# Expert places ordered by token counts, with rooms of 448, 416 or 384 tokens, in 26 blocks instead of 28

## The chip, the core and the metric

The kernel runs on one NeuronCore of a Trainium2 chip. TensorE multiplies matrices into PSUM, VectorE and ScalarE work elementwise, GpSimd works elementwise and also issues the indirect transfers (rows picked by a list of indices), SyncE issues most plain transfers. The engines run beside each other and wait for each other by semaphores. The metric is the device time of one execution in microseconds, the median of several. Lower is better.

## What is computed

A gated linear attention is followed by a mixture of experts, in which each token goes to the one expert with the largest logit:

```python
# attention, (B, H, S, D) = (4, 8, 768, 48); its output is x, 3072 tokens of 384 numbers
state = alpha[:, :, t, :, None] * state + np.einsum('bhd,bhe->bhde', k[:, :, t], v[:, :, t])
y[:, :, t] = np.einsum('bhd,bhde->bhe', q[:, :, t], state)

# experts, N, D, E, F = (3072, 384, 8, 1024)
logits = x @ w_gate
expert_idx = np.argmax(logits, axis=1)
...                                    # probs = softmax(logits)
gate_w = probs[np.arange(N), expert_idx]
for e in range(E):                     # over the tokens of expert e
    h = np.maximum(x_sorted[lo:hi] @ w1[e], 0.0)
    y_sorted[lo:hi] = h @ w2[e]
y = y_sorted[inv_perm]
return gate_w[:, None] * y
```

All of it is float32. How many tokens an expert gets is known only when the logits are there, on the chip.

## The kernel before

The attention goes through 24 blocks of 128 tokens. Each block's rows and logits go to a table `x_rows` in memory. Beside it the kernel finds each token's expert and its slot, a number that says where in the experts' rows the token stands. A pair of experts shares 7 blocks of 128 slots: the first expert fills them from the front, the second from the back, each with room for 448 tokens, so the middle block is half of one and half of the other. A slot is cut into its row (0 to 127) and its column (the block), each made into a one-hot, and a matmul of the two writes the token's number where its slot is:

```python
    EP = E // 2; NJ = 7; HB = C // 2; CAP = NJ * HB      # C = 128: CAP = 448
    NX = -(-(N - CAP) // C); PB = NX + NJ + NX; NC = EP * PB   # NC = 196 columns

    def one_hots(s, eng=nc.vector):
        rc = st[s]["rc"]
        eng.tensor_scalar(oh_r[:, s, :], iota_h[:, :C], scalar1=rc[:, 0, :], scalar2=None, op0=ALU.is_equal)
        eng.tensor_scalar(oh_c[:, s, :], iota_h[:], scalar1=rc[:, 1, :], scalar2=tokv[:, s : s + 1],
                          op0=ALU.is_equal, op1=ALU.mult)

    def tokens_of_slots(t0, t1):
        for t in range(t0, t1):
            nc.tensor.matmul(route[:, :NC], lhsT=oh_r[:, t, :], rhs=oh_c[:, t, :], ...)

    def indices():
        tv = route[:, :NC]
        nc.vector.tensor_scalar_add(g_mid[...], tv[... NX : NX + NJ], float(N // 2))
        ...                                     # g_idx (all columns) and o_idx (rows of the output)
```

Between the last attention block and the first expert stand these steps. `keep_busy(n)` is n matmuls on zeros, whose result nobody reads:

```python
        one_hots(hots.pop(0), nc.gpsimd)
        one_hots(hots.pop(0))
        tokens_of_slots(9, NT - 3)
        slots_of(*rank_products(groups_of[-1], ...))
        tokens_of_slots(NT - 3, NT - 1)
        keep_busy(3)
        one_hots(hots.pop(0))
        tokens_of_slots(NT - 1, NT)
        nc.tensor.matmul(route[:, NC : NC + E], lhsT=ones_sq[:], rhs=ohs[:, NT, :], ...)
        keep_busy(8)
        indices()
```

Then the experts. A gather brings 128 rows of a block, `turn` transposes them on TensorE and VectorE copies them into `xT`, layer 1 multiplies with `w1` over the whole room of the expert, and layer 2 multiplies block by block with `w2`. The result is scaled by the gate and scattered to the output:

```python
    def products1(w1, xT, hp, f, c0, c1):
        for a in range(DB):                                   # DB = 3
            nc.tensor.matmul(hp[:, c0:c1], lhsT=w1[:, a, f * C : (f + 1) * C], rhs=xT[:, a, c0:c1], ...)

    def layer1(w1, xT, cols, begun=(), c0=0, then=None):      # cols = CAP
        h = wk.tile([C, FB, CAP], F32, name="h_sb")
        for f in range(FB):                                   # FB = 8
            hp = ...                                          # one of 3 PSUM tiles
            products1(w1, xT, hp, f, ..., cols)
            ...                                               # relu, VectorE for even f, ScalarE for odd f

    def layer2(parts, gw, idx, apart):
        zp = mps.tile([C, Dm], F32, name="zp")
        m = C // len(parts)                                   # 128, or 64 in the shared block
        for f in range(FB):
            for i, (w2, h, c0) in enumerate(parts):
                nc.tensor.matmul(zp[i * m : (i + 1) * m, :], lhsT=h[:, f, c0 : c0 + m], rhs=w2[:, f, :], ...)
        ...                                                   # scale on ScalarE, scatter on GpSimd

    xg = gather(columns(0))
    for p in range(EP):
        a, b = 2 * p, 2 * p + 1
        ...                                                   # fetches of weights, gather of the next pair
        ha = layer1(w_t[a][0], xTa, CAP, begun, 2 * C)
        for j in range(NH + 1, NJ):                           # NH = 3
            turn(xg, j, (xTb, HB + (j - NH - 1) * C, 0, C))
        gw = gates(xg, NJ)
        for j in range(NH):
            layer2([(w_t[a][1], ha, j * C)], gw[:, j : j + 1], idx[j], True)
        hb = layer1(w_t[b][0], xTb, CAP)
        ...                                                   # turns of the next pair; for p == 0 extra_blocks()
        layer2([(w_t[a][1], ha, NH * C), (w_t[b][1], hb, 0)], gw[:, NH : NH + 1], idx[NH], True)
        for j in range(NH + 1, NJ):
            layer2([(w_t[b][1], hb, HB + (j - NH - 1) * C)], gw[:, j : j + 1], idx[j], True)
```

`extra_blocks` works out, on VectorE, how many tokens don't fit into their expert's room; a loop at the end runs once per block of such tokens.

Of the kernel before, what the change touches and what calls it, by code (L numbers as in the profile page):

```python
# [8 lines left out]
F32 = mybir.dt.float32  # L9
# [9 lines left out]
def kernel(  # L19
# [24 lines left out]

    nc = tc.nc
    B, H, S, D = q.shape
    C = 128
# [13 lines left out]
    EP = E // 2  # L61
    NJ = 7
    HB = C // 2
    CAP = NJ * HB

    NX = -(-(N - CAP) // C)
    PB = NX + NJ + NX
    NC = EP * PB

    W = Dm + E  # L70

    ends = list(range(0, NT - 7, 4)) + [NT - 5, NT - 3, NT - 1, NT]
    groups_of = [range(a, b) for a, b in zip(ends, ends[1:])]

# [43 lines left out]
    zero_w = consts.tile([1, W], F32)  # L118
    iotas = {}
    for name, shape, dt, pattern, base, mult in (  # L120

        ("first_w", [C, E], F32, [[-1, E]], E, 0),
        ("iota_h", [C, NC], F16, [[1, NC]], 0, 0),

        ("tokv", [C, NT], F32, [[N // 2 + 1, 2], [C, NT // 2]], -(N // 2), 1),
        ("sgn", [C, E], F32, [[0, EP], [2, 2]], -1, 0),
        ("slot0", [C, E], F32, [[PB * C, EP], [1, 2]], NX * C + CAP - 1, 0),

        ("base2", [C, E], F32, [[2 * PB, EP], [0, 2]], 2 * NX + NJ, 0),
        ("thr", [C, NX], F32, [[C, NX]], CAP, 0),  # L130
        ("kx", [1, NX], F32, [[1, NX]], 0, 0),
        ("xcol", [1, E], F32, [[PB, EP], [NJ + 1, 2]], NX - 1, 0),
    ):
        iotas[name] = (
            consts.tile(shape, I32, name=name + "_i"), consts.tile(shape, dt, name=name), pattern, base, mult,
        )
    first_w, iota_h, tokv, sgn, slot0, base2, thr, kx, xcol = (iotas[n][1] for n in iotas)

    def late_consts(i):
# [10 lines left out]
        if i in (2, 3, 4):  # L150
            for ti, tf, pattern, base, mult in list(iotas.values())[3 * (i - 2) : 3 * (i - 1)]:
                nc.gpsimd.iota(ti[:], pattern=pattern, base=base, channel_multiplier=mult)
                nc.gpsimd.tensor_copy(tf[:], ti[:])
            if i == 3:
                nc.gpsimd.tensor_scalar_mul(ohs[:, 0, :], base2[:], 0.5)
                first = ohs[0:1, 0, :].rearrange("p (a b) -> p a b", b=2)[:, :, 0]
                nc.gpsimd.tensor_scalar_add(first, first, -1.0)
            if i == 2:

                nc.sync.dma_start(x_d[N // 2 : N // 2 + 1, :], zero_w[:])  # L160

# [10 lines left out]

    g_mid = rte.tile([C, EP * NJ], I32)
    g_idx = rte.tile([C, NC], I32)
    o_idx = rte.tile([C, NC], I32)
    tot = rte.tile([C, E], F32)
# [38 lines left out]
    with tc.tile_pool(name="ld", bufs=6) as ld, \  # L215
# [35 lines left out]
        def cums(s):  # L251
            d = st[s]
            cum = ps.tile([C, Dm], F32, name="cum")
# [124 lines left out]
        def choose(g):  # L378
# [8 lines left out]

            if n == 1:
                nc.vector.scalar_tensor_tensor(
                    oh[:, t, :], in0=sc[:], scalar=top[:], in1=sgn[:, None, :], op0=ALU.is_equal, op1=ALU.mult,  # L390
                )
            else:
                nc.vector.tensor_tensor(sc[:], sc[:], top[:].unsqueeze(2).to_broadcast([C, n, E]), op=ALU.is_equal)
                nc.vector.tensor_tensor(oh[:, t, :], sc[:], sgn[:, None, :].to_broadcast([C, n, E]), op=ALU.mult)
# [10 lines left out]
        def slots_of(g, pos):  # L405
# [4 lines left out]
            slot_i = work.tile([C, n], I32, name="slot_i")  # L410
            with nc.allow_low_precision("a single number is not zero, and it is an integer"):
                nc.vector.tensor_reduce(slot_i[:], own[:], axis=AX, op=ALU.add, apply_absolute_value=True)
            rc_i = work.tile([C, 2, n], I32, name="rc_i")
            nc.vector.tensor_scalar(rc_i[:, 0, :], slot_i[:], scalar1=C - 1, scalar2=None, op0=ALU.bitwise_and)
            nc.vector.tensor_scalar(rc_i[:, 1, :], slot_i[:], scalar1=7, scalar2=None, op0=ALU.arith_shift_right)
            rc = work.tile([C, 2, n], F32, name="rc")
            nc.vector.tensor_copy(rc[:], rc_i[:])
            for i, s in enumerate(g):
                st[s]["rc"] = rc[:, :, i : i + 1]
                hots.append(s)  # L420

        def one_hots(s, eng=nc.vector):
            rc = st[s]["rc"]
            eng.tensor_scalar(oh_r[:, s, :], iota_h[:, :C], scalar1=rc[:, 0, :], scalar2=None, op0=ALU.is_equal)
# [12 lines left out]
        def indices():  # L437

            tv = route[:, :NC]
            nc.vector.tensor_scalar_add(  # L440
                g_mid[:].rearrange("p (a b) -> p a b", a=EP),
                tv.rearrange("p (a b) -> p a b", a=EP)[:, :, NX : NX + NJ], float(N // 2),
            )
            nc.vector.tensor_scalar_add(g_idx[:], tv, float(N // 2))
            up = [work.tile([C, NC], F32, name="up") for _ in range(2)]
            nc.vector.tensor_scalar(up[0][:], tv, scalar1=0.0, scalar2=-1.0, op0=ALU.is_gt, op1=ALU.mult)
            nc.vector.tensor_scalar(up[1][:], tv, scalar1=0.0, scalar2=float(N), op0=ALU.is_equal, op1=ALU.mult)
            nc.vector.tensor_tensor(up[0][:], up[0][:], up[1][:], op=ALU.add)
            nc.vector.scalar_tensor_tensor(
                o_idx[:], in0=tv, scalar=float(N // 2), in1=up[0][:], op0=ALU.add, op1=ALU.add,  # L450
            )
# [65 lines left out]
        route = ps.tile([C, Dm], F32, name="cum")  # L517
# [11 lines left out]
        tokens_of_slots(NT - 3, NT - 1)  # L529
        keep_busy(3)  # L530
        one_hots(hots.pop(0))
        tokens_of_slots(NT - 1, NT)
# [4 lines left out]
        indices()  # L537
        nc.vector.tensor_copy(tot[:], route[:, NC : NC + E])
# [6 lines left out]

    def extra_blocks():

        cnt = sm.tile([C, E], F32)
        nc.vector.tensor_tensor(cnt[:], tot[:], slot0[:], op=ALU.subtract)
        nc.vector.tensor_tensor(cnt[:], cnt[:], sgn[:], op=ALU.mult)  # L550
        og = sm.tile([C, E, NX], F32)
        nc.vector.tensor_tensor(
            og[:], cnt[:].unsqueeze(2).to_broadcast([C, E, NX]), thr[:, None, :].to_broadcast([C, E, NX]), op=ALU.is_gt,
        )
        ovt = sm.tile([C, E], F32)
        nc.vector.reduce_sum(ovt[:], og[:], axis=AX)
        ove = sm.tile([C, E], F32)
        nc.vector.tensor_tensor_scan(ove[:], ovt[:], zero_e[:], 0.0, op0=ALU.add, op1=ALU.add)
        ovs = sm.tile([1, E], F32)
        nc.vector.tensor_sub(ovs[:], ove[0:1, :], ovt[0:1, :])  # L560
# [11 lines left out]
        nth = sm.tile([1, NX, E], F32)  # L572
        nc.vector.tensor_tensor(nth[:], kx_b, per(ovs), op=ALU.subtract)
        live = sm.tile([1, NX, E], F32)
        nc.vector.tensor_scalar(live[:], nth[:], scalar1=0.0, scalar2=None, op0=ALU.is_ge)
        nc.vector.tensor_tensor(live[:], live[:], ended[:], op=ALU.subtract)
        nc.vector.tensor_tensor(nth[:], nth[:], per(sgn), op=ALU.mult)
        nc.vector.tensor_tensor(nth[:], nth[:], per(xcol), op=ALU.add)
        nc.vector.tensor_tensor(nth[:], nth[:], live[:], op=ALU.mult)
        nc.vector.reduce_sum(xf[:, NX : 2 * NX], nth[:], axis=AX)  # L580
# [3 lines left out]
    def gather(idx, n=0, later=False):  # L584

        xg = xg_pools[n % 2].tile([C, len(idx), W], F32, name="xg")
        if later:

            nc.vector.memset(xg[:, 0, :1], 0.0)
        for j, i in enumerate(idx):  # L590
            nc.gpsimd.indirect_dma_start(  # L591
# [36 lines left out]
    def layer1(w1, xT, cols, begun=(), c0=0, then=None):  # L628
        h = wk.tile([C, FB, CAP], F32, name="h_sb")
        for f in range(FB):  # L630
# [6 lines left out]
            if f == 0 and then:  # L637
                done = then()
        return (h, done) if then else h
# [129 lines left out]
```

## Time and profile before

| | |
|---|---|
| time, median of 3 | 473.68 us (472.63 to 473.82) |
| span of the profiled execution | 473.3 us |
| TensorE busy | 452.8 us (96%), 2919 matmul instructions |
| VectorE, ScalarE, GpSimd busy | 144.7, 106.0, 141.2 us |
| layer 2 (L647), busy | 146.8 us, 512 matmul instructions |
| layer 1 (L620), busy | 145.9 us, 402 matmul instructions |
| gathers (L591), scatters (L653) | 28 and 28 |
| moved by DMA | 59.79 MB |

In the profile's lines PE is TensorE's matmuls, PEld its loads of weights, DVE VectorE, ACT ScalarE, POOL GpSimd, SP SyncE; L620 is line 620 of the kernel. Shapes are partitions x elements, xcount is how many instructions a line stands for, and a bracket at the end of a timeline's line is how long the engine sat idle before it and what ended that. PEclk is the share of full clock that TensorE was granted. The lengths of matmuls overlap, as they are pipelined: the pace is read from start to start.

### The profile page before, as it was taken

To read this page: it belongs to the slowest core of one execution; us is meant where nothing else is said; L and a number is where in the kernel's file an instruction comes from. 1 tells how busy PE (TensorE), PEld (TensorE's weight loads), DVE (VectorE), ACT (ScalarE), POOL (GpSimd) and SP (SyncE) were. 2 spreads that over 40 slices of the span, in tenths; PEclk is the share of its full clock that TensorE was granted. 3 is DMA by queue.
4 is the path that set the end of the run, shared out by engine and by line. 5 is a ranking of instruction groups with operands and counts; after the bars stand their busy time and mean duration, and the time that the engine had idled before them with its cause. 6 is when DMAs were issued, how large, how long until landed. Compare 5 with 4: busy or idle time off the path is not lost.

```text
span 473.3 us, 7538 instructions
## 1 busy us (share of the span) xinstructions
PE 452.8 (96%) x2919; PEld 294.2 (62%) x2919; DVE 144.7 (31%) x412; ACT 106.0 (22%) x209; POOL 141.2 (30%) x228
## 2 busy tenths in 40 slices
PE   8999999999997899999999999999999999999992
PEld 5787887888886765554555555555555554555451
DVE  2646776767776312015013012001201101201000
ACT  3554554555531011010011010010110001111100
POOL 4567565556643500250160100133010010010020
PEclk9999999999999999999999999999999999999998
DMA  9999999999433404974473202634400230000000
GB/s 163 190 197 189 207 198 204 214 210 206 102 102 119 116 5 171 392 268 145 172 227 103 86 18 81 218 123 151 144 33 1 67 115 13 1 21 17 1 35 26
DMA packets 128687, 59.79 MB, mean 126 GB/s; under 512 B 110624, under 2 KB 123460, under 8 KB 128650
## 3 DMA queue, kind: packets, MB, share of 16 engines
q1 hardware_dynamic: 116258, 48.87, 41.1%
q0 software_dynamic: 3584, 10.34, 6.5%
q10 hardware_dynamic: 8808, 0.08, 1.1%
q8 instruction: 24, 0.39, 0.4%
q14 instruction: 13, 0.11, 0.1%
HBM read 49.70 MB, written 10.35 MB: 127 GB/s over the span
## 4 chain that ended last, share of the span: by engine, by line
issue 48%; PE 29%; POOL 10%; DMA 4%; DVE 3%; SPq 3%; ACTq 1%; ACT 1%; POOLq 0%
POOL out_dram L653 5%; PE hp L620 4%; POOL xg L591 4%; PE sA L298 4%; PE xr L365 3%; PE tp L285 3%; PE zp L647 3%; PE cum L254 3%; PE y L335 2%; PE y L328 2%; DMA x_rows<-xs 2%; DMA k_sb<-in_k_dram 2%; SPq L233 2%; PE kvp L335 2%; PE kvp L344 1%
## 5 line engine op out<-in xcount | busy, mean ns | idle before, releaser
L647 PE MATMUL zp<-w,h_sb 128*128 128x384 f32 (+1 forms) x512 | 146.8, 488 | 0.0
L620 PE MATMUL hp<-xT,w 128*128 128x448 f32 (+2 forms) x402 | 145.9, 523 | 0.6 <-DVE xT L616 0.6
L647 PEld LDWEIGHTS zp<-w,h_sb 128*128 128x128 f32 (+1 forms) x512 | 81.2, 177 | 62.3 <-issue 13.6
L620 PEld LDWEIGHTS hp<-xT,w 128*128 128x128 f32 x402 | 75.7, 190 | 68.3 <-issue 65.0
L653 POOL DMA_INDIRECT out_dram<-zo,o_idx x28 | 27.8, 992 | 246.9 <-ACT zo L652 246.9
L634 DVE TENSOR_SCALAR h_sb<-hp 128x448 f32<-128x448 f32 x32 | 20.0, 625 | 218.3 <-PE hp L620 206.7
L636 ACT ACTIVATE h_sb<-hp 128x448 f32<-128x448 f32 x32 | 17.4, 545 | 139.8 <-PE hp L620 131.9
L652 ACT ACTIVATE zo<-zp,gw 128x384 f32<-128x384 f32 x28 | 16.3, 582 | 133.5 <-PE zp L647 128.9
L591 POOL DMA_INDIRECT xg<-x_rows,g_mid x28 | 27.0, 966 | 12.9 <-issue 7.3
L298 PE MATMUL sB<-qT,kT 48*128 48x128 f32 x192 | 27.7, 285 | 0.0
L298 PE MATMUL sA<-qT,kT 48*128 48x128 f32 x192 | 27.7, 284 | 0.0
L285 PEld LDWEIGHTS tp<-ident,kqb 128*128 128x128 f32 x192 | 22.4, 140 | 7.2 <-issue 4.2
L277 POOL TENSOR_TENSOR kqb<-k_sb,icp 128x384 f32<-128x384 f32 x24 | 24.0, 1002 | 9.5 <-ACT icp L257 7.5
L365 PE MATMUL xr<-back,yT 128*128 128x104 f32 x192 | 25.1, 273 | 0.0
L285 PE MATMUL tp<-ident,kqb 128*128 128x128 f32 x192 | 24.9, 273 | 0.0
L254 PE MATMUL cum<-ln,cmask 128*128 128x384 f32 x48 | 22.0, 540 | 3.0 <-ACT ln L243 2.9
L298 PEld LDWEIGHTS sA<-qT,kT 48*128 48x128 f32 x192 | 23.1, 187 | 2.0 <-issue 0.5
L278 POOL TENSOR_TENSOR kqb<-q_sb,cp 128x384 f32<-128x384 f32 x24 | 24.1, 1003 | 0.0
L365 PEld LDWEIGHTS xr<-back,yT 128*128 128x128 f32 x192 | 23.3, 192 | 0.1
L298 PEld LDWEIGHTS sB<-qT,kT 48*128 48x128 f32 x192 | 23.1, 187 | 0.0
L305 POOL TENSOR_SCALAR_AFFINE_SELECT dB<-dB 128x512 f32<-128x512 f32 x24 | 15.3, 637 | 22.7 <-ACT dB L304 22.7
L616 DVE COPY xT<-xtp 128x384 f32<-128x384 f32 (+1 forms) x32 | 14.9, 504 | 21.8 <-PE xtp L614 21.8
(138 smaller groups left out, 456.1 us busy)
## 6 DMA issues: line engine op xcount, KB each, us to landing
w<-in_moe_w_dram SPq DMA_DIRECT2D x14, 1536.0 KB
x_rows<-xs SPq DMA_DIRECT2D x24, 196.0 KB
a_sb<-in_alpha_dram SPq DMA_DIRECT2D x24, 192.0 KB
k_sb<-in_k_dram SPq DMA_DIRECT2D x24, 192.0 KB
q_sb<-in_q_dram SPq DMA_DIRECT2D x24, 192.0 KB
vb<-in_v_dram SPq DMA_DIRECT2D x24, 192.0 KB
w<-in_moe_w_dram SPq DMA_DIRECT2D x12, 128.0 KB
w<-in_moe_w_dram SPq DMA_DIRECT2D x8, 192.0 KB
```

The source lines that it names most:

```text
L254: nc.tensor.matmul(cum[:], lhsT=cmask[:], rhs=d["ln"][:], start=True, stop=True)
L277: nc.gpsimd.tensor_tensor(kq[:, 0, :, :D], d["k"][:], heads(d["icp"]), op=ALU.mult)
L278: nc.gpsimd.tensor_tensor(kq[:, 1, :, :D], d["q"][:], heads(d["cp"]), op=ALU.mult)
L285: nc.tensor.transpose(tp[:, p, :], pair(kqb[s % 4][:, i], p), ident[:])
L298: nc.tensor.matmul(t[:, p, :], lhsT=d["kT"][r : r + D, p, :], rhs=d["qT"][r : r + D, p, :], start=True, stop=True,)
L335: nc.tensor.matmul(yp(p)[at(p, a) : at(p, a) + DP, :], lhsT=d["v"][:, 2 * p + a, :], rhs=d["d" + "AB"[a]][:, p, :], start=(c == 0 and p % ...
L365: nc.tensor.matmul(xr[:, p, :], lhsT=d["yT"][:, p, :], rhs=back[:, p, :], start=True, stop=True)
L591: nc.gpsimd.indirect_dma_start(out=xg[:, j, :], out_offset=None, in_=x_d[:, :], in_offset=bass.IndirectOffsetOnAxis(ap=i, axis=0),)
L620: nc.tensor.matmul(hp[:, c0:c1], lhsT=w1[:, a, f * C : (f + 1) * C], rhs=xT[:, a, c0:c1], start=(a == 0), stop=(a == DB - 1), skip_group_c ...
L634: nc.vector.tensor_relu(h[:, f, :cols], hp[:, :cols])
L647: nc.tensor.matmul(zp[i * m : (i + 1) * m, :], lhsT=h[:, f, c0 : c0 + m], rhs=w2[:, f, :], start=(f == 0), stop=(f == FB - 1), skip_group_ ...
L653: ins = nc.gpsimd.indirect_dma_start(out=out[:, :], out_offset=bass.IndirectOffsetOnAxis(ap=idx, axis=0), in_=zo[:], in_offset=None, bound ...
```

## The change

Instead of pairs with 448 slots for everyone, the eight experts get places in a row, with rooms of 448, 384, 448, 384, 416, 416, 416 and 416 slots: 3328 slots, which are 26 blocks of 128. Expert 0 has the first place; the other seven are put into the places by the order of their token counts, which the chip takes from the ranks after 19 of the 24 blocks (`turns`). The aim is fewer empty slots to compute. As the rooms are multiples of 32, a slot is cut into units of 32, and a block can belong to two experts in parts of 64 and 64 or of 32 and 96. Layer 2 then cuts a shared block into tiles of the smaller part. Which expert stands in a place is read from memory into a register, of SyncE for the fetches of weights and of VectorE for the indices. The diff, cut to what matters:

```diff
-    EP = E // 2
-    NJ = 7
-    HB = C // 2
-    CAP = NJ * HB
+    UN = 32
+    NQ = C // UN
+    NU = 16
+    NC = E * NU
+    caps = (448, 384, 448, 384, 416, 416, 416, 416)
+    nth_of = (5, 0, 6, 1, 2, 3, 4)
+    begins = [sum(caps[:i]) for i in range(E + 1)]
+    NBK = begins[-1] // C
...
+        def turns(first):
+            key = ...                    # count * 8 + tie, of experts 1 to 7, on one partition
+            ...                          # stand = how many have a larger key, by a 7 x 7 comparison
+            nc.vector.tensor_reduce(order_i[:], cmp[:], axis=AX, op=ALU.add)
...
         def one_hots(s, eng=nc.vector):
-            eng.tensor_scalar(oh_r[:, s, :], iota_h[:, :C], scalar1=rc[:, 0, :], scalar2=None, op0=ALU.is_equal)
+            eng.tensor_scalar(oh_r[:, s, :], iota_r[:], scalar1=rc[:, 0, :], scalar2=None, op0=ALU.is_equal)
...
-        def indices():
...
+        def slots(i):
+            b, n = begins[i] // UN, caps[i] // UN
+            tv = route[:, :NC].rearrange("p (e k q) -> p e k q", e=E, q=NQ)
+            e = nc.vector.value_load(order_i[0:1, i - 1 : i], min_val=1, max_val=E - 1) if i else 0
+            for q in range(NQ):
+                ...
+                to, src = g_idx[r, k : k + m], tv[r, bass.ds(e, 1), :m, u]
+                if i == 0 and q % 2:
+                    nc.scalar.activation(to, src, AF.Copy, bias=float(N // 2))
+                else:
+                    nc.vector.tensor_scalar_add(to, src, float(N // 2))
...
         tokens_of_slots(9, NT - 3)
         slots_of(...)
-        tokens_of_slots(NT - 3, NT - 1)
-        keep_busy(3)
+        keep_busy(4)
         one_hots(hots.pop(0))
-        tokens_of_slots(NT - 1, NT)
+        tokens_of_slots(NT - 3, NT)
         nc.tensor.matmul(route[:, NC : NC + E], ...)
         keep_busy(8)
-        indices()
+        slots(0)
...
     def layer2(parts, gw, idx, apart):
-        m = C // len(parts)
+        wd = C if len(parts) == 1 else min(m for *_, m in parts)
+        cuts = [(w2, h, c) for w2, h, c0, m in parts for c in range(c0, c0 + m, wd)]
         for f in range(FB):
-            for i, (w2, h, c0) in enumerate(parts):
-                nc.tensor.matmul(zp[i * m : (i + 1) * m, :], lhsT=h[:, f, c0 : c0 + m], ...)
+            for i, (w2, h, c) in enumerate(cuts):
+                nc.tensor.matmul(zp[i * wd : (i + 1) * wd, :], lhsT=h[:, f, c : c + wd], ...)
...
+    lots = [range(a, b) for a, b in ((0, 7), (7, 13), (13, 20), (20, NBK))]
+    def weights1(i, later=False):
+        nos[i] = nc.sync.value_load(order_i[0:1, i - 1 : i], min_val=1, max_val=E - 1)
+        w1n[i] = fetch1(nos[i], later)
+    ended = [range(begins[i] // C, begins[i + 1] // C) for i in range(E)]
+    needed = [range(-(-begins[i] // C), -(-begins[i + 1] // C)) for i in range(E)]
+    fetch_lot(0, {begins[i] // C: i for i in (1, 2)})     # slots(1) ahead of gather 3, slots(2) ahead of 6
+    for i in range(E):
+        ...
+        h_t[i] = layer1(w_t[i][0], xT[i], caps[i], begun, 2 * C)
+        if i + 1 < E:
+            for k in needed[i + 1]:
+                turn_block(k)
+        if i == 0:
+            ...                                            # weights of places 1 and 2
+            gates_lot(0)
+            for n in range(3, E):
+                slots(n)
+            rows_out(o_idx[:], g_idx[:])
+        if i + 3 < E:
+            weights1(i + 3)
+        for n, k in enumerate(ended[i]):
+            ...                                            # gates of a new lot
+            results(k)                                     # layer 2 of block k
+            if n == 0 and i and i + 2 < E:
+                weights2(i + 2)
+        if i in (0, 1, 3):
+            fetch_lot((0, 1, None, 2)[i] + 1)
+        if i == 0:
+            ...
+            extra_blocks()
```

`extra_blocks` is adapted to the rooms, and the token numbers of the overflow loop are now made only when that loop runs.

## The prediction

> **What bounds the kernel now.** I read three views. The first is the busy time by stage: I cut the span where the work changes, at 147 us (the attention blocks end), 161.25 us (the first expert product), and then at the edges of the first expert pair.
>
> ```profile
> core 0: us, PE busy (x) PEld busy (x) DVE busy (x) ACT busy (x) POOL busy (x), PEclk, DMA share, GB/s
> 100.00:147.00 47.00, 46.66 (x670) 40.49 (x668) 35.30 (x108) 21.55 (x45) 25.26 (x49) 1.00 0.64 146
> 147.00:161.25 14.25, 10.47 (x56) 8.20 (x57) 6.98 (x32) 0.48 (x1) 6.92 (x10) 0.88 0.34 98
> 161.25:181.60 20.35, 20.03 (x81) 13.60 (x82) 4.66 (x9) 2.18 (x4) 2.32 (x3) 1.00 0.13 39
> 238.10:314.00 75.90, 75.25 (x246) 40.81 (x245) 9.61 (x21) 8.69 (x16) 13.64 (x14) 1.00 0.34 117
> 390.00:464.50 74.50, 74.17 (x235) 39.47 (x233) 7.50 (x16) 8.69 (x16) 6.90 (x7) 1.00 0.05 16
> 464.50:473.30 8.80, 0.00 (x0) 0.00 (x0) 0.00 (x0) 0.58 (x1) 0.98 (x1) 0.79 0.04 13
> ```
>
> From 161 us on TensorE is busy at full clock in practically the whole of every stretch, while VectorE and GpSimd idle most of it and the DMA share falls to a third or less. So the expert stage is **TensorE's own pace**, and each column of matmul left out there shortens the run. Ahead of it lies a junction of 14.25 us with a granted clock of 0.88, behind it a tail of 8.80 us without matmuls.
>
> The second view is TensorE's timeline, for the pace of each part of an expert.
>
> ```profile
> 180.10 0.82 PE L614 MATMUL xtp<-ident,xg 128*128 128x128 f32 x6
> 181.62 15.65 PE L647 MATMUL zp<-w,h_sb 128*128 128x384 f32 x48
> 197.10 18.20 PE L620 MATMUL hp<-xT,w 128*128 128x448 f32 x48
> 215.14 0.82 PE L614 MATMUL xtp<-ident,xg 128*128 128x128 f32 x6
> 217.23 21.06 PE L647 MATMUL zp<-w,h_sb 128*64 128x384 f32 x80
> 238.12 18.20 PE L620 MATMUL hp<-xT,w 128*128 128x448 f32 x48
> ```
>
> Columns are start, length, instruction, count. Every f32 matmul of the source stands there as two passes (8 x 3 products are x48). Layer 1 of one expert goes from 197.10 to 215.14: 18.04 us for 48 passes, 0.376 us a pass, **0.84 ns a column**. Three blocks of layer 2 go from 181.62 to 197.10: 15.48 us, 5.16 a block, 0.3225 us a pass, again 0.84 ns a column. The x80 are the shared block, done as two halves of 64 columns, and three full blocks: 20.89 us to the next line's start, less 15.48, leaves **5.4 us for a block in halves**, so two half-width tiles run side by side at almost no loss. Turning three blocks costs 181.62 - 180.10 = 1.52 us, four 2.09.
>
> The third view is the timeline of the junction, TensorE, then VectorE's and GpSimd's first step after it.
>
> ```profile
> 149.81 0.17 PE L402 MATMUL sB<-oh,lt_strict 128*128 128x8 f16 x1 [0.31 <-DVE oh L389]
> 151.89 0.33 PE L432 MATMUL cum<-oh_c,oh_r 128*128 128x196 f16 x2 [1.92 <-POOL oh_c L425]
> 152.06 2.67 PE L462 MATMUL xr<-still 128*128 128x256 f32 x6
> 154.53 0.37 PE L432 MATMUL cum<-oh_c,oh_r 128*128 128x196 f16 x1
> 154.79 4.11 PE L462 MATMUL xr<-still 128*128 128x256 f32 x16
> ```
>
> ```profile
> 154.94 0.19 DVE L440 TENSOR_SCALAR g_mid<-cum 128x28 int32<-128x28 f32 x1 [3.35 <-PE cum L533]
> ```
>
> ```profile
> 155.44 1.23 POOL L591 DMA_INDIRECT xg<-x_rows,g_mid  x1 [3.60 <-DVE g_mid L440]
> ```
>
> TensorE waits 1.92 us for GpSimd's one-hot, then runs six filler passes in 2.67 us, that is 0.445 us a pass where 256 columns at 0.84 ns would take 0.215: it has dropped to half pace. VectorE's last one-hot was ready at 151.60, but its product stands behind these fillers and starts at 154.53. The fillers are on the path to the first gather.
>
> **What the Trainium skill says.** *TensorEngine Tiling (Array Packing)*, "Available Configurations", lists 128x64 with two tiles and 128x32 with four. The trace agrees for two (5.4 us above); of four 32-wide tiles it shows nothing. It does show four 64x64 tiles at once: the 16 passes of L328 over 128 columns take 0.60 us where one after the other they would take 16 x 0.107 = 1.7. "Key Properties" of the same page says that a change of tiling mode drains TensorE; that fits the 0.24 us by which a halved block exceeds a full one. *TensorE: Matmul & The Clock Gate*, "What's actually happening", says that the clock halves after about 3.4 us without enough work; the 0.445 us pass and the 0.88 agree with halving. *DMA: Bandwidth & Descriptors*, "Latency and other measured facts", gives a register load from memory a floor of some 600 ns; no line before shows one by itself.
>
> **The change, part by part.**
>
> *Do the tokens fit?* If an expert outgrows its room the overflow loop runs, which would cost tens of us. The reference's inputs are fixed, so I worked the counts out: 420, 387, 356, 354, 404, 409, 352, 390. The order is taken from the first 19 of 24 blocks (counts 333, 301, 288, 270, 332, 325, 282, 301), which gives places 0, 6, 4, 3, 5, 1, 7, 2 with counts 420, 352, 404, 354, 409, 387, 390, 356 in rooms of 448, 384, 448, 384, 416, 416, 416, 416. All fit, so the loop stays empty as before.
>
> *Layer 1.* Per expert 48 passes x columns x 0.84 ns: 18.06 us at 448, 16.77 at 416, 15.48 at 384. Before, 8 x 18.06 = 144.5. After, 2 x 18.06 + 4 x 16.77 + 2 x 15.48 = 134.2. **-10.3 us.**
>
> *Layer 2.* Before, 24 blocks x 5.16 + 4 x 5.4 = 145.4. After, 26 blocks. The places begin at 448, 832, 1280, 1664, 2080, 2496, 2912; against multiples of 128 the remainders are 64, 64, 0, 0, 32, 64, 96. So three blocks are in halves and two in 32 and 96, cut into four tiles of 32: 21 x 5.16 + 3 x 5.4 + 2 x 5.8 = 136.2. The 5.8 is my estimate: four side by side, with twice the weight loads of a halved block, so I let the excess over 5.16 grow from 0.24 to about 0.6. **-9.2 us.**
>
> *Turning.* After the first four blocks, four threes and three fours (12.4 us) become six threes and one four (11.2). **-1.2 us.** A shared block now needs two copies on VectorE as before.
>
> *Junction.* The fillers move ahead of the last one-hots: 8 passes start at about 150.0, where TensorE now idles, and end at 151.7 at full pace or 153.5 at half. The one-hots are 128 wide, not 196, so GpSimd's 1.02 us one shrinks to perhaps 0.75 and ends near 151.6. Then three short products, some 0.5 us, and the indices of place 0: two operations on VectorE and two on ScalarE, about 0.4 us in place of 0.19. The first gather starts at 153.2 (full pace) or 155.0 (half), against 155.44. I choose **-1.8 us**, nearer to full pace, as the idle 1.92 us is filled. The two register loads ahead of gathers 3 and 6 take perhaps 1 to 1.5 us each; gather 3 is due some 4 us after the first, so VectorE has time.
>
> *What lands beside other work.* Five further register loads, 20 small index operations, the row computation and the overflow arithmetic fall on VectorE during expert 0's layer 2: 5 x (1.2 + 0.8) + 1.5 + 6 = 17 us by estimate, against 15.5 us of layer 2 on TensorE. The first relu of the next layer 1 is due 2 us into it and three hidden tiles give another 4 us, so it nearly fits; I put down **+0.8 us** for a stall. Weights by register change the issue alone; their DMA is slack. Attention keeps its operations; VectorE loses some one-hot width there, off its limit. The tail stays at 8.8 us.
>
> Sum: -10.3 - 9.2 - 1.2 - 1.8 + 0.8 = -21.7 us, from 473.7 to **452.0 us**.
>
> **The rivals.**
>
> *Four narrow tiles don't run side by side.* With two at a time each of the two blocks takes 10.3 us: +9, so 461. One after the other, 64 passes x 0.3225 = 20.6 us: +30, so 482. For it: nothing before has tiles of 32 columns. Against: the four at once of L328, and the halves. 8% for the first kind, 3% for the second.
>
> *VectorE becomes the bound in the first expert.* If a register load holds it for 3 us and not 1.2, the seven cost 13 us more; five of them push the relu of expert 1 some 9 us late, of which TensorE's slack takes part: +4 to +8, so 456 to 460. For it: all of it is on one in-order engine. Against: VectorE is busy only 1.55 us of the 15.50 between 181.60 and 197.10.
>
> *Weights or rows arrive late.* A shorter expert gives less time for 3.1 MB of weights and a gather. The DMA share of 0.34 over a pair of experts, 9% shorter, speaks against it: +0 to +3.
>
> *The junction is worth nothing or more:* between 0 and -3 us.
>
> **Range and chances.** All columns saved and a full junction would give 449; a stall and somewhat slower narrow tiles give 456 to 458. I take 448.5 to 458.0. Within 2% means above 464.2, which needs the first rival together with another: 5%. Slower by over 2% (483.2) needs fully serial tiles and more: 3%. Faster by over 2%: 92%.
>
> **What would show each step right or wrong.** Relu groups of 448, 416 and 384 columns with TensorE passes of 0.376, 0.349 and 0.3225 us; 26 scatters and 26 gathers; shared blocks 16 and 22 near 5.8 us (10 or 20 would be the first rival); the first gather near 153.5; no wait of TensorE for VectorE near the second expert's start longer than 1 us. The prediction falls if the expert stage is not some 20 us shorter, or if attention, which I leave alone, moves by more than 2 us.

## The result, and the profile after

The changed kernel takes **449.4 us** (median of 4, 447.9 to 450.8), where the kernel before takes 473.75 us in the same session. The ratio is 0.948, with a 95% interval of 0.944 to 0.953. The predicted time was 452.0 us, with a range of 448.5 to 458.0.

First the same cut by stage as before. The columns are the stretch and its length, then for each engine busy time and number of instructions, the granted clock of TensorE, the DMA share and GB/s. The edges are again the first hidden product, here 156.66 us, and the end of the last layer-2 product, here 440.25; behind it lies the tail of 8.65 us.

```profile
core 0: us, PE busy (x) PEld busy (x) DVE busy (x) ACT busy (x) POOL busy (x), PEclk, DMA share, GB/s
...
145.00:156.66 11.66, 8.70 (x58) 7.11 (x58) 6.51 (x35) 0.81 (x3) 6.43 (x10) 0.99 0.43 123
156.66:177.00 20.34, 20.34 (x72) 13.80 (x73) 3.59 (x7) 1.63 (x3) 2.34 (x3) 0.92 0.14 38
177.00:440.25 263.25, 260.99 (x963) 144.91 (x961) 40.53 (x124) 30.21 (x58) 43.04 (x44) 1.00 0.34 116
```

From 177 us on TensorE is still the engine without gaps. Place 0 (156.66 to 177.00) now has a granted clock of 0.92, where the kernel before had 1.00; the junction has 0.99 where it had 0.88. In this pair of profiles the half pace has moved from the one to the other; the experiments and the account of the prediction show how much of that is chance.

Next TensorE's timeline in the experts: two places with 384 and 416 slots, and the two blocks of the 32 and 96 kind.

```profile
178.55 15.65 PE L730 MATMUL zp<-w,h_sb 128*128 128x384 f32 x48
194.03 15.64 PE L704 MATMUL hp<-xT,w 128*128 128x384 f32 x48
...
211.13 15.90 PE L730 MATMUL zp<-w,h_sb 128*64 128x384 f32 x64
226.86 18.20 PE L704 MATMUL hp<-xT,w 128*128 128x448 f32 x48
...
300.37 16.92 PE L704 MATMUL hp<-xT,w 128*128 128x416 f32 x48
317.13 0.82 PE L698 MATMUL xtp<-ident,xg 128*128 128x128 f32 x6
...
352.52 15.89 PE L730 MATMUL zp<-w,h_sb 128*32 128x384 f32 x96
368.24 16.92 PE L704 MATMUL hp<-xT,w 128*128 128x416 f32 x48
```

Start to start, layer 1 with 416 columns takes 317.13 - 300.37 = 16.76 us. The x64 at 211.13 are one block in halves (32 passes) and two full blocks: 226.86 - 211.13 = 15.73 us, less 2 x 5.16, leaves 5.41. The x96 at 352.52 are one block in four tiles of 32 (64 passes) and two full ones: 368.24 - 352.52 = 15.72, which leaves **5.40 us for the block in four tiles**, the same as for halves.

Last the junction: TensorE first, then the indices of place 0 on VectorE and ScalarE, and the first gather.

```profile
147.62 0.17 PE L427 MATMUL sB<-oh,lt_strict 128*128 128x8 f16 x1 [0.60 <-DVE oh L419]
147.65 1.97 PE L507 MATMUL xr<-still 128*128 128x256 f32 x8
149.46 0.33 PE L478 MATMUL cum<-oh_c,oh_r 128*128 128x128 f16 x3
...
149.68 3.72 PE L507 MATMUL xr<-still 128*128 128x256 f32 x16
154.30 0.52 PE L698 MATMUL xtp<-ident,xg 128*128 128x128 f32 x3 [0.90 <-DMA xg<-x_rows,g_idx]
155.47 0.55 PE L698 MATMUL xtp<-ident,xg 128*128 128x128 f32 x3 [0.65 <-DMA xg<-x_rows,g_idx]
156.66 4.37 PE L704 MATMUL hp<-xT,w 128*128 128x256 f32 x12 [0.65 <-DVE xT L700]
```

```profile
149.83 0.15 DVE L496 TENSOR_SCALAR g_idx<-cum 32x4 int32<-32x4 f32 x1 [0.47 <-PE cum L577]
150.22 0.16 DVE L496 TENSOR_SCALAR g_idx<-cum 32x3 int32<-32x3 f32 x1 [0.23 <-ACT g_idx L494]
```

```profile
150.02 0.17 ACT L494 ACTIVATE g_idx<-cum 32x4 int32<-32x4 f32 x1 [2.80 <-DVE g_idx L496]
150.41 0.17 ACT L494 ACTIVATE g_idx<-cum 32x3 int32<-32x3 f32 x1 [0.22 <-DVE g_idx L496]
```

```profile
150.87 1.22 POOL L675 DMA_INDIRECT xg<-x_rows,g_idx  x1 [1.56 <-ACT g_idx L494]
```

The eight filler passes run at full pace (1.97 us, next product after 1.81) and the last products come behind them without a wait. The four index operations, divided between two engines, do not run beside each other: each bracket names the other engine, and they take 0.75 us together. The first 12 hidden passes take 4.37 us, where the kernel before took 2.86: half pace, after two turns (three passes each) with waits between them.

The difference of the two profiled spans, 473.3 - 448.9 = 24.4 us, divides so:

| stretch | before | after | difference |
|---|---|---|---|
| start to the last rank product | 149.81 | 147.62 | -2.2 |
| to the first gather | 5.63 | 3.25 | -2.4 |
| to the first hidden product | 5.81 | 5.79 | 0.0 |
| to the end of the last layer-2 product | 303.25 | 283.59 | -19.7 |
| tail | 8.80 | 8.65 | -0.1 |

### The profile page after: what moved, and what is told of

Read it like the earlier page. It is cut to its first block, busy times and chain, and to the rows that moved or that the text cites. A ratio compares the mean times of both kernels' runs of the same rounds, so it can differ in the third digit from the quotient of the medians.

```text
span 448.9 us, 7761 instructions
## 1 busy us (share of the span) xinstructions
PE 431.3 (96%) x2963; PEld 286.3 (64%) x2963; DVE 146.4 (33%) x443; ACT 104.1 (23%) x209; POOL 138.7 (31%) x245
## 3 DMA queue, kind: packets, MB, share of 16 engines
q0 software_dynamic: 3328, 9.94, 6.8%
## 4 chain that ended last, share of the span: by engine, by line
PE 73%; issue 11%; DMA 5%; POOL 4%; DVE 3%; ACT 1%; SPq 1%; ACTq 0%; POOLq 0%
PE hp L704 27%; PE zp L730 23%; PE sA L330 3%; PE tp L317 3%; PE cum L286 3%; PE xr L397 3%; DMA x_rows<-xs 2%; PE y L367 2%; PE xtp L698 2%; PE y L360 2%; POOL out_dram L736 2%; PE kvp L367 1%; PE xr L507 1%; PE kvp L376 1%; DMA k_sb<-in_k_dram 1%
## 5 line engine op out<-in xcount | busy, mean ns | idle before, releaser
L704 PE MATMUL hp<-xT,w 128*128 128x416 f32 (+4 forms) x402 | 137.2, 502 | 0.6 <-DVE xT L700 0.6
L730 PE MATMUL zp<-w,h_sb 128*128 128x384 f32 (+2 forms) x560 | 136.7, 488 | 0.0
L704 PEld LDWEIGHTS hp<-xT,w 128*128 128x128 f32 x402 | 76.8, 193 | 58.8 <-issue 43.0
L730 PEld LDWEIGHTS zp<-w,h_sb 128*128 128x128 f32 (+2 forms) x560 | 73.8, 162 | 59.6 <-issue 17.2
L736 POOL DMA_INDIRECT out_dram<-zo,o_idx x26 | 25.8, 993 | 232.7 <-ACT zo L735 165.6
L718 DVE TENSOR_SCALAR h_sb<-hp 128x416 f32<-128x416 f32 (+2 forms) x32 | 18.9, 592 | 183.1 <-PE hp L704 183.1
L720 ACT ACTIVATE h_sb<-hp 128x416 f32<-128x416 f32 (+2 forms) x32 | 16.6, 517 | 125.9 <-PE hp L704 125.9
L735 ACT ACTIVATE zo<-zp,gw 128x384 f32<-128x384 f32 x26 | 15.1, 581 | 127.9 <-PE zp L730 123.4
L675 POOL DMA_INDIRECT xg<-x_rows,g_idx x26 | 25.1, 966 | 9.2 <-issue 7.0
L320 DVE COPY qT<-tp 128x512 f32<-128x512 f32 x24 | 16.5, 687 | 15.7 <-PE tp L317 15.3
```

The lines of the kernel that those rows point to most:

```text
L675: nc.gpsimd.indirect_dma_start(out=xg[:, j, :], out_offset=None, in_=x_d[:, :], in_offset=bass.IndirectOffsetOnAxis(ap=i, axis=0),)
L718: nc.vector.tensor_relu(h[:, f, :cols], hp[:, :cols])
L720: nc.scalar.activation(h[:, f, :cols], hp[:, :cols], AF.Relu)
L730: nc.tensor.matmul(zp[i * wd : (i + 1) * wd, :], lhsT=h[:, f, c : c + wd], rhs=w2[:, f, :], start=(f == 0), stop=(f == FB - 1), skip_group ...
L736: ins = nc.gpsimd.indirect_dma_start(out=out[:, :], out_offset=bass.IndirectOffsetOnAxis(ap=idx, axis=0), in_=zo[:], in_offset=None, bound ...
```

## The experiments

All times in one paragraph are from the same chip; ratios are to the kernel before on that chip.

### Both kernels profiled again

No edit.

> The kernel before, profiled once more. The matmuls of the attention ran 0.88 us earlier in the changed kernel from block 0, 1.6 us from block 7 and 1.9 to 2.2 us from block 14 on, though the change leaves them alone. Theory A (chance: the loads of the attention are bound by DMA and don't always fall alike): the last xr of the attention, at 147.35 us in the first profile, moves by 1 us or more in this repeat. Theory B (the change shortens the attention): it stays within 0.4 us of 147.35.

> The changed kernel, profiled once more. Theory A (chance in the attention): its last xr, at 145.23 us in the first profile, moves by 1 us or more here or in the repeat of the kernel before. Theory B (the change shortens the attention): within 0.4 us of 145.23, so again 2.1 us ahead of the kernel before. In both: the stretch from the first hidden product to the last layer-2 product stays at 283.6 us.

The repeats, one run each, took 476.1 and 449.0 us. The last xr of the attention starts at 148.96 us in the repeat of the kernel before and at 144.98 in that of the changed kernel. Each moves a little (1.6 and 0.25 us), so there is chance in it, as theory A has it: in the repeat of the kernel before, TensorE had half the clock from 82.54 to 85.96 us, in the middle of the attention. But the two don't mix. Over all profiles of this study with the attention of the kernel before it starts at 147.35, 148.96, 147.31 and 148.27 us (the third and fourth are variants told of below); over all ten with that of the change at 143.7 to 146.4. The means are 148.0 and 145.2. **Chance alone is refuted; the change shortens the attention, by 2.7 us in the means**, by something I had not counted. The starts of the cumulative sums show where: at block 2 12.99 to 13.07 us in the four and 11.90 to 12.54 in the ten, at block 7 41.30 to 41.44 and 39.34 to 40.13. So about 1.5 us of it is there by block 7.

From the first hidden product to the end of layer 2 the repeat of the changed kernel takes 282.07 us, not 283.59. Its first 12 passes take 2.86 us, not 4.37, and that is the whole difference: the half pace at the start of place 0 comes in some executions and not in others.

### Rooms of 448 for everybody

```diff
-    caps = (448, 384, 448, 384, 416, 416, 416, 416)
+    caps = (448,) * 8
-    lots = [range(a, b) for a, b in ((0, 7), (7, 13), (13, 20), (20, NBK))]
+    lots = [range(a, b) for a, b in ((0, 7), (7, 14), (14, 21), (21, NBK))]
-    fetch_lot(0, {begins[i] // C: i for i in (1, 2)})
+    fetch_lot(0, {begins[1] // C: 1})
-            for n in range(3, E):
+            for n in range(2, E):              # slots(2) is made with those of places 3 to 7
                 slots(n)
```

> The changed kernel with a room of 448 for every place, so 28 blocks again: the rooms undone, everything else kept (order, registers, single indices, fillers). Theory (the rooms are the gain): layer 1 gives back 10.3 us, layer 2 some 10.1, turning 1.2, so 449.4 + 21.6 = 471 us, a ratio of about 0.994 to the kernel before. Rival (the order, the registers or the junction hold a good part of the gain, or the added index work costs something that the rooms hide): below 465, or above 474.

470.9 us, ratio 0.990 (0.987 to 0.992), on a chip where the kernel before takes 475.9. The rooms undone give back 21.9 us against the changed kernel's 449.0 there (a single run). The stretch of the experts is that of the kernel before to the hundredth:

```profile
155.20:458.45 303.25, 300.98 (x992) 165.55 (x992) 46.74 (x136) 34.11 (x63) 49.10 (x51) 1.00 0.31 105
```

303.25 us in both. So neither the order, nor the registers, nor the single index operations cost or bring anything in the experts: **all of that stage's gain is work that TensorE no longer does**: columns of layer 1, blocks of layer 2 and their turns. What stays of the gain, 5.0 us by the times, lies before the experts.

### All blocks in narrow tiles

```diff
-        wd = C if len(parts) == 1 else min(m for *_, m in parts)
+        wd = UN                                # 32
```

> The changed kernel with layer 2 of all 26 blocks cut into four tiles of 32 columns, not only of the two blocks that need it. Same products, four times the matmul instructions in 21 blocks. Theory A (four narrow tiles run side by side, and the 0.24 us of a shared block is the change of shape): 0.24 us for each of the 8 experts at most, less the five blocks that have it now, so 449.4 to 451.5 us. Theory B (the 0.24 us comes from loading more weights in every such block): 21 x 0.24 = +5.0, so 454.4. Rival (narrow tiles run at a lower pace once they follow each other block after block): a quarter slower would be 21 x 1.3 = +27 us, 476.

451.25 us, ratio 0.948 (0.945 to 0.950), on the chip of the last paragraph. Three narrow blocks in a row, and what follows:

```profile
179.64 15.69 PE L730 MATMUL zp<-w,h_sb 128*32 128x384 f32 x192
195.26 15.75 PE L704 MATMUL hp<-xT,w 128*128 128x384 f32 x48
210.84 0.82 PE L698 MATMUL xtp<-ident,xg 128*128 128x128 f32 x6
```

Start to start 195.26 - 179.64 = 15.62 us for three blocks with four times the instructions, against 15.48 in full tiles: 0.05 us a block. The layer 1 that follows takes 15.58 in place of 15.48. That is theory A: most of the 0.24 us of a shared block is paid where the shape changes, in and out, and not for the weights. Four f32 tiles of 32 columns run side by side, block after block, at almost full pace.

### The fillers put back

```diff
         slots_of(*rank_products(groups_of[-1], ...))
-        keep_busy(4)
-        one_hots(hots.pop(0))
-        tokens_of_slots(NT - 3, NT)
+        tokens_of_slots(NT - 3, NT - 1)
+        keep_busy(3)
+        one_hots(hots.pop(0))
+        tokens_of_slots(NT - 1, NT)
```

> The changed kernel with the order of the junction put back: two products of one-hots, three fillers, the last one-hots, the last product. Theory (the fillers were on the path, at half pace): the first gather starts some 2 us later after the last rank product (3.25 us in the changed kernel, 5.6 in the kernel before), time 451.0 to 451.8. Rival (the first gather is held by something else, such as the last rows landing in memory, or the fillers now run at full pace): less than 0.7 us slower.

452.3 us, ratio 0.951 (0.948 to 0.954). From the last rank product to the first gather it takes 4.50 us, not 3.25. The theory holds in direction, the size is 1.25 us and not 2, for here the three fillers run at full pace. The time alone would not show it: the changed kernel was not timed on this chip, and its ratios elsewhere are 0.948 and 0.950.

```profile
149.74 0.27 PE L478 MATMUL cum<-oh_c,oh_r 128*128 128x128 f16 x2 [1.56 <-POOL oh_c L471]
149.85 1.51 PE L507 MATMUL xr<-still 128*128 128x256 f32 x6
151.19 0.22 PE L478 MATMUL cum<-oh_c,oh_r 128*128 128x128 f16 x1
```

Six passes take 1.51 us, where in the kernel before they took 2.67, so an execution with half pace here would lose about 1.2 us more (an estimate from these two).

### The fillers alone, in the kernel before

The reverse edit, in the kernel before, which keeps its pairs, its rooms and its 196-column one-hots.

```diff
-        tokens_of_slots(NT - 3, NT - 1)
-        keep_busy(3)
+        keep_busy(4)
         one_hots(hots.pop(0))
-        tokens_of_slots(NT - 1, NT)
+        tokens_of_slots(NT - 3, NT)
```

> The kernel before with only the order of the junction changed: four fillers ahead of the last one-hots, then the three products together. Theory (the fillers were on the path): 2.0 to 2.4 us faster than the kernel before at the first gather, less what TensorE loses by starting the experts at half pace, so a ratio of 0.995 to 0.998. Rival (this part brings its gain only together with the narrower one-hots): a ratio of 0.999 to 1.001.

472.8 us on the chip of the last paragraph, where the kernel before takes 475.4: ratio 0.996 (0.994 to 0.998). From the last rank product to the first gather it takes 2.92 us, against 5.63, 4.98 and 5.77 in three profiles with the old order. The lines are the last rank product, the fillers, the last products and the gather:

```profile
149.76 0.17 PE L402 MATMUL sB<-oh,lt_strict 128*128 128x8 f16 x1 [0.31 <-DVE oh L389]
149.78 1.97 PE L462 MATMUL xr<-still 128*128 128x256 f32 x8
151.73 0.41 PE L432 MATMUL cum<-oh_c,oh_r 128*128 128x196 f16 x3
```

```profile
152.68 1.23 POOL L590 DMA_INDIRECT xg<-x_rows,g_mid  x1 [1.00 <-DVE g_mid L440]
```

Its first 12 hidden passes run at full pace, in 2.86 us. This part of the change is a gain by itself. The stretch is even a little shorter than the changed kernel's 3.25 us, where four alternating index operations take 0.75 us and here one takes 0.19.

### One-hots as wide as before

```diff
-    NU = 16
+    NU = 24                                    # NC = 192 columns
```

> The changed kernel with 24 units per expert, so one-hots of 192 columns, near the 196 of the kernel before, in place of 128. Theory (narrower one-hots freed VectorE and GpSimd, and this is why the attention ended about 2 us earlier): last xr at 147 us or later, time some 2 us up, 451.5. Rival (one-hot width is beside the path, the attention's difference is chance): last xr within the spread of the repeats, and only the junction slower by 0.2 to 0.4 us, time 449.6 to 449.9.

451.0 us, ratio 0.950 (0.946 to 0.954), on the same chip. The last xr starts at 145.39 us, in the middle of the ten; from the last rank product to the gather it takes 3.44 us, not 3.25. By the trace the rival holds: the width costs 0.2 us in the junction, and **the shorter attention does not come from it**. The time, which the theory put at 451.5 and the rival at 449.6 to 449.9, decides nothing, as the changed kernel was not timed on this chip.

### GpSimd's constants spread, in the kernel before

```diff
-        if i in (2, 3, 4):
-            for ti, tf, pattern, base, mult in list(iotas.values())[3 * (i - 2) : 3 * (i - 1)]:
+        steps = {2: ("first_w", "sgn"), 3: ("base2", "iota_h"), 4: ("tokv", "slot0"), 5: ("thr", "kx"), 6: ("xcol",)}
+        if i in steps:
+            for ti, tf, pattern, base, mult in [iotas[n] for n in steps[i]]:
```

> The kernel before with GpSimd's constants spread as in the change: two per block over five blocks, where it made three per block in three blocks. Theory (these constants held up block 7 of the attention: the start of its cumulative sum came 6.3 to 6.9 us after block 6's in the kernel before and 5.8 to 6.1 in the changed one): the two steps to blocks 6 and 7 together fall from 12.5 us to about 12.0, the attention ends 0.5 to 0.8 us earlier than at 147.3, ratio 0.998 to 0.999. Rival (it is the loads or where tiles lie): both steps stay at 12.5, ratio 1.000.

475.0 us against 475.8, ratio 0.999 (0.997 to 1.001). The two steps to blocks 6 and 7 together take 6.16 + 6.42 = 12.58 us, as they did (5.75 + 6.85 = 12.60). The edit brought nothing, but it doesn't refute the theory either, for it left as much work standing at the decisive place. Before block 7 TensorE's first rank product (`kvp`) needs GpSimd's running sums (`ohs`). Here are GpSimd's copy to `xs`, its sums and that product, first in this run, then in the changed kernel:

```profile
38.78 0.19 POOL L374 COPY xs<-lgn 128x8 f32<-128x8 f32 x1 [0.22 <-DMA x_rows<-xs]
40.59 1.03 POOL L397 TENSOR_TENSOR ohs<-ohs,oh 128x8 f16<-128x8 f16 x4
41.39 0.18 PE L402 MATMUL kvp<-ohs,ones_sq 128*128 128x32 f16 x1 [0.55 <-POOL ohs L397]
```

```profile
37.69 0.19 POOL L405 COPY xs<-lgn 128x8 f32<-128x8 f32 x1 [0.48 <-DVE sc L416]
38.95 1.04 POOL L421 TENSOR_TENSOR ohs<-ohs,oh 128x8 f16<-128x8 f16 x4
39.76 0.18 PE L426 MATMUL kvp<-ohs,ones_sq 128*128 128x32 f16 x1 [0.28 <-POOL ohs L421]
```

Between the copy and the sums stand constants and, in the old attention, two operations that give the sums their first value: 1.62 us here and 1.77 to 1.80 in the other three profiles with it, against 1.07 to 1.18 in the ten with the change, which sets that value a block earlier. TensorE waits 0.46 to 0.98 us for the sums in the four and at most 0.28 in the ten. So GpSimd's work there is part of why block 7 comes earlier; no run took it away by itself.

The profile of this run shows one thing more: its first 12 hidden passes took 4.54 us, so the kernel before can start the experts at half pace too.

### Place indices made three times over

```diff
-            for n in range(3, E):
+            for n in [*range(3, E)] * 3:
                 slots(n)
```

> The changed kernel with the indices of places 3 to 7 made three times over, each with its register load: VectorE has 10 such groups more, 12.4 us by the 1.24 us that one takes, between the first gates and the overflow arithmetic. Theory (VectorE is in order and has little slack there): its arithmetic ends at about 205.4 us in place of 193.0, the first relu of place 1 comes after it, TensorE runs out of hidden tiles three products groups into that layer and waits some 6 us, time 455 to 456. Rival (the slack takes it): under 451.

456.5 us, where the changed kernel takes 451.3 on the same chip. VectorE ends its arithmetic at 205.2 us, and TensorE's second layer 1 breaks in two:

```profile
193.28 7.90 PE L704 MATMUL hp<-xT,w 128*128 128x384 f32 x24
205.73 10.19 PE L704 MATMUL hp<-xT,w 128*128 128x384 f32 x24 [4.55 <-DVE h_sb L718]
```

The wait is 4.55 us, and after it the 24 passes take 10.0 us in place of 7.7, again half pace behind a gap (the granted clock is 0.50 from 203.35 to 210.17 us). Four of the eight hidden tiles got through before it, not three as I had counted. So this limit is real, and the changed kernel is on its near side: there VectorE is idle for 2.96 us before the relu in question, as this line of the changed kernel's timeline shows.

```profile
196.17 0.56 DVE L718 TENSOR_SCALAR h_sb<-hp 128x384 f32<-128x384 f32 x1 [2.96 <-PE hp L704]
```

### Fillers between the first turns

```diff
+            begun = [hidden_tile() for _ in range(3)]
+            fill(begun[2], 2)                  # matmuls on zeros, 256 columns, overwritten later
             turn_block(0)
+            fill(begun[2], 2)
             turn_block(1)
-            begun = [hidden_tile() for _ in range(3)]
+            fill(begun[2], 2)
```

> The changed kernel with fillers of 256 columns ahead of, between and behind the first two turns (two each, on a PSUM tile that the products overwrite), where TensorE waits for the gathers. Theory (the first 12 hidden products took 4.37 us and not 2.6 as the clock had halved in these waits): they take 2.6 to 3.0 us, and time falls by 1 to 1.5 us, to 448. Rival (the clock halves whatever runs there, or the fillers push the turns back by as much as they save): no change within 0.4 us, or slower.

449.3 us, ratio 0.946 (0.943 to 0.949), on the chip of the two experiments on fillers. The first 12 hidden passes take 2.81 us:

```profile
155.62 1.03 PE L796 MATMUL hp<-still 128*128 128x256 f32 x4
156.49 2.81 PE L704 MATMUL hp<-xT,w 128*128 128x256 f32 x12
```

They start 5.95 us after the first gather, as against 5.79 and 5.87, so the fillers hold the turns back by some 0.1 us. The changed kernel was not timed on that chip, so both ran once more together.

> The changed kernel once more, on the chip of the version with fillers, to compare the two: 449 to 450 us. Its first 12 hidden products took 4.37 us once and 2.86 us once, so runs should lie in two groups some 1.5 us apart.

> The version with fillers between the first turns, once more beside the changed kernel. Theory (it makes the full pace at the first products certain): the median lies 0.5 to 1 us below the changed kernel's on the same chip. Rival: within 0.3 us.

451.3 us for the changed kernel (six runs, 449.4 to 453.5; ratio 0.950, 0.947 to 0.953) and **449.6 us with the fillers** (448.0 to 450.6; ratio 0.946, 0.943 to 0.949). The medians are 1.7 us apart, where 1.5 us of half pace in most executions would give somewhat less, and the passes again took 2.81 us. The two intervals overlap slightly, so the gain is likely and its size not settled. The two groups of times that I expected of the changed kernel are not to be seen; the six spread evenly. Its profile had the slow start (4.54 us).

## Why the prediction was right

The time was right, and in the experts and the junction the mechanism too: -21.7 us predicted, -24.4 in the profiles. What failed is the step on the attention. Luck has a part in the sum: two terms that were not foreseen, -2.2 and +1.5, partly cancel, and 449.4 us lies only 0.9 above the lower end of the range. By its steps, in us:

| step | predicted | measured |
|---|---|---|
| layer 1 | -10.3 | as predicted: 15.48, 16.76 and 18.04 a place |
| layer 2 | -9.2 | -10.0: full blocks 5.16, halves 5.41, four tiles 5.40 |
| turning | -1.2 | -0.8 |
| junction | -1.8 | -2.4 |
| stall on VectorE | +0.8 | 0 |
| half pace at the start of place 0 | not foreseen | +1.5 in this profile |
| attention | 0 | -2.2 |
| tail | 0 | -0.1 |

*Layer 1* was exact, because its pace was read from two column counts before it was used for a third.

*Layer 2.* The term that was mis-sized is the block in four tiles: 5.8 us by my guess that its excess grows with the number of weight loads. It is 5.40 us, and the run with narrow tiles everywhere shows that most of the excess belongs to the change of shape. The first rival, tiles that don't run side by side, is refuted by the same run.

*Turning* gave back less: three blocks take 1.53 us where a full block follows, and 1.62 where a shared one does (211.13 - 209.51), which I had not set apart.

*Junction.* The step was right in kind, and full pace was the better of its two cases: the fillers now fill a wait in which TensorE had dropped to half pace. The gain of the old kernel with this order alone, 2.1 to 2.9 us in the trace, shows it. But 0.75 us for the indices was twice my 0.4, as the two engines take turns.

*VectorE as the bound* did not come about. A group of one register load and four operations takes 1.23 us and not 2.0: from 181.36 to 182.59 and so on, five in a row.

```profile
181.36 0.68 DVE L496 TENSOR_SCALAR g_idx<-cum 32x3 int32 x4 [0.63 <-issue]
182.59 0.67 DVE L496 TENSOR_SCALAR g_idx<-cum 32x4 int32 x4 [0.56 <-issue]
183.82 0.67 DVE L496 TENSOR_SCALAR g_idx<-cum 32x3 int32 x4 [0.56 <-issue]
```

The bracket, 0.56 to 0.63 us, is time in which VectorE computes nothing. The load is only a part of it, as a view of its source line shows (shortest, median and longest in ns; the 552 is the first of the seven):

```profile
L487 DVEq TENSOR_LOAD <-order_i x7: 301/309/552, 150.2 to 185.5; - x7
```

The Trainium skill gives `tensor_load` a floor of some 600 ns (*DMA: Bandwidth & Descriptors*, "Latency and other measured facts"), and the prediction allowed 1.2 us for a load; here six of seven took 0.30 to 0.34 us, and the measurement decides. The trace of the kernel before has such a load on VectorE too, of 0.54 us at 441.76, which the prediction overlooked. The block of index work and overflow arithmetic took 12.5 us (180.73 to 193.21) where I had put 17.

*Half pace at the start of place 0* was not in the sum. The prediction had the experts start at full pace, as they had before. In the twelve profiles without fillers at that place the 12 passes took 2.86 us five times and 4.3 to 4.5 us seven times. The traces show what decides. In all 14 profiles, TensorE's granted clock changes only at the edges of steps of 3.41 us, which lie elsewhere in each execution, and up to the end of layer 2 a fall to half lasts one step, once two. Here are steps of the changed kernel's first profile, of its repeat, and of the version with fillers:

```profile
152.93:156.34 3.41, 1.53 (x9) 1.00 0.59 163
156.34:159.76 3.42, 3.10 (x7) 0.50 0.62 161
```

```profile
151.04:154.45 3.41, 2.46 (x13) 1.00 0.39 98
154.45:157.86 3.41, 2.09 (x11) 1.00 0.59 155
157.86:161.28 3.42, 3.42 (x20) 1.00 0.56 161
```

```profile
151.59:155.01 3.42, 3.36 (x17) 1.00 0.47 124
155.01:158.42 3.41, 3.41 (x19) 1.00 0.58 169
```

The columns are the step and its length, TensorE's busy time and passes, the granted clock, the DMA share and GB/s. In the first profile one step falls wholly into the wait for the gathers, is busy for 1.53 us, and the next has half the clock. In the repeat the edge at 154.45 cuts the wait in two, and the clock stays. Of the 1814 steps in the 14 profiles up to the end of layer 2, the 13 ahead of a step at half clock have 1.03 to 1.85 us of busy TensorE by the profile, turns included, and all others 2.00 or more. *TensorE: Matmul & The Clock Gate*, "What's actually happening", tells of such a window of about 3.4 us that runs on its own count, and these steps agree. So where the edges lie in an execution decides, which is chance, and fillers that keep the step of the wait busy (3.36 us) take that chance away. The half pace of the junction in the kernel before is the same thing: the step from 148.78 to 152.19, with the wait of 1.92 us, is busy for 1.18 us.

*Attention* was to stay within 2 us, and it moved by 2.2 in the first pair, which by the prediction's own sign counts against it. The step that failed is "Attention keeps its operations": the change also moves the first value of GpSimd's running sums a block ahead, spreads GpSimd's constants, takes the multiplication by a sign out of VectorE's work on the ranks and gives the cumulative sum a PSUM pool of its own. Shown is that TensorE waited for GpSimd's sums at block 7 before and hardly waits after. It is not the rooms (143.72 us with all at 448) and not the width of the one-hots. How much each of the others brings (and where tiles lie in memory, and the loads' issue on SyncE) **was not tried and stays open**.

## What to carry to other kernels

When a trace shows one engine without gaps and a pace that is the same for two sizes, work left out on that engine comes back in full, and its price can be read before anything is built: here 0.84 ns for each column of each pass. Rooms may then be cut to sizes that are awkward for blocks, as a block in four narrow tiles costs little beyond the change of shape. These rooms fit these token counts; no run here shows what an expert that outgrows its room would cost. Beside it, look at what stands in an in-order queue ahead of a short critical step: fillers moved from behind a wait into it gave over 2 us in the kernel before without leaving any work out.

## What was not expected of the hardware

- An f32 block in four tiles of 32 columns, with four times the instructions, takes 5.40 us among full blocks (5.16) and 5.2 among its like.
- The same wait of about 3 us halves TensorE's clock in some executions and not in others (4.3 to 4.5 us or 2.86 us for the same 12 passes), by where the edges of steps of 3.41 us fall: in these traces a step with 1.85 us of busy time or less is followed by one at half clock, a step with 2.00 or more is not.
- Small operations on two engines that write parts of one tile took turns, with about 0.2 us from one's start to the other's, and were no faster than four in a row on one engine (0.67 us). By the brackets each waited for the other, so the turns may be the program's own; whether the engines could run them together was not tried.
